# A decode step of attention and feed-forward: half-length result rows stored by ScalarE, block transposes on VectorE, and wo in one load

## The chip, the cores and the metric

One core of one Trainium2 chip. The metric is the device time of one execution in microseconds (us); lower is better. The profiler also gives a *span*, from the first to the last recorded instruction of the program; the time is longer than the span by what the chip does ahead of it and behind it.

## The reference

One token for each of two sequences passes through a transformer block whose layer norms are modulated by a condition `c`. All tensors are bf16; D = 640, 32 heads of 192, the last 1024 of 4096 cached keys and values, F = 1536.

```
mod = (silu(c) @ w_mod).reshape(2, 6, 1, 640)        # sa, ca, ga, sb, cb, gb
h = layernorm(x) * (1 + ca) + sa
x = x + ga * attention(h, k_cache, v_cache, wq, wo)
h = layernorm(x) * (1 + cb) + sb
x = x + gb * ((gelu(h @ w_gate) * (h @ w_up)) @ w_down)
```

## The kernel before

Every weight and every cached key and value is read once, through one arena in SBUF and one queue of loads issued by SyncE. A load is issued as soon as what its place held is consumed; waits for semaphores are worked out from a list of reads and writes. Results with one row for each sequence are laid out as four blocks of 160 columns at partitions 32i, with sequence b at partition 32i + 16b: so TensorE can run four products at once, one at each of its four column positions (in the trace the four matmuls of a round start within 0.01 us of each other).

The parts that the change touches (cuts marked with ...):

```python
WO_SPLIT = [(0, 39), (39, 9)]                         # wo in two loads
...
def f(e):                                             # LN output to columns: 20 small matmuls, then a cast
    hv = hrow[:, :].rearrange("p (m j) -> p m j", j=KT)
    for j in range(KT):
        for i in range(NR):
            last = e.matmul(ps[32*i:32*i+32, BK_M, CT+2*j:CT+2*j+2], lhsT=hv[:, :, j], rhs=selrow[:, i, :], ...)
S.op("dve", lambda e: e.tensor_copy(out=dst_bf[:, :, :], in_=ps[:, BK_M, CT:CT+2*KT]...), ...)
...
keep_clock(9, "clock0")                               # matmuls whose only use is to keep TensorE's clock up
for ci, (t0, n) in enumerate(WO_SPLIT):               # attention output @ wo: 96 matmuls of 320 columns
    ...
    for bk, lo, w in ((2, 0, NA), (3, NA, NA)):
        last = e.matmul(ps[32*i:32*i+B, bk, 0:w], lhsT=oT[:, t, :], rhs=wv[:, tl, lo:lo+w], ...)
# wS <- PSUM by ScalarE and VectorE, then a product with selw sums the four blocks into rows
...
wk = wv[:, k, :].rearrange("p (m i r) -> p i m r", i=NR, r=FR)      # gate and up read runs of 3 of every 12
last = e.matmul(ps[32*i:32*i+B, bk, 0:FT]..., lhsT=h2T[:, k, :], rhs=wk[:, i, :, :], ...)
...
for i in range(NR):                                   # down: 48 matmuls of 160 columns
    last = e.matmul(ps[32*i:32*i+RM, BK_OT, CY:CY+DR], lhsT=aT[:, fc, :], rhs=wv[:, i, :], ...)
S.op("dve", ... fin = ps * modR[:, 5, :]); S.op("dve", ... finb = fin + X)
S.dma("sp", k_dma(out[:, 0, :].rearrange("b (i n) -> i b n", i=NR), finb[0:P:RB, :]), sem_out, ...)
...
S.emit("sp", nc.sync, tail=lambda e: e.wait_ge(sem_out, 16))        # SyncE waits for the store
```

## Time and profile before

| | us |
|---|---|
| time, median of 3 runs | 185.97 (185.91 to 186.12) |
| span of the profiled run | 184.9 |
| last weight landing (semaphore record) | 182.05 |
| from there to the end of the span | 2.8 |

The profile is read in three steps, whose lines stand in the prediction below. The row of DMA activity says whether the stream of loads ever pauses. The chain that ended last, in order of time, says what stands behind the last landing. The timeline of the last 20 us says what runs beside the end of the stream and how long each piece waits; a figure in brackets is idle time ahead of a piece, with what ended it. One more record is used, though no view prints it: each load raises its semaphore in 16 parts (16 records for each load in these traces), which are read here as one for each of the core's 16 DMA engines. A consumer waits for all 16.

### The profile page before, as it was taken

The page shows a single profiled execution, that of the slowest core. Times are in us where ns is not written, and L with a number is a line of the kernel's source. Part 1 is how long each engine was busy: PE and PEld are TensorE (multiplying, and loading weights), DVE is VectorE, ACT ScalarE, POOL GpSimd, SP SyncE. Part 2 cuts the span into 40 slices and gives each one's busy share as a digit, 9 for nine tenths or more (in the row PEclk, how much of TensorE's full clock was granted, in tenths as well). Part 3 has the DMA queues.
Part 4 walks back from the last instruction along what each step waited for, and adds up shares of the span by engine and source line. Part 5 has one row for each costly group of instructions (what it writes and reads, how often), then busy time and mean ns, then how long its engine had stood idle before and what let it go on. Part 6 is the DMA issues. An engine that isn't in the chain of part 4 may idle for free.

```text
span 184.9 us, 1610 instructions
## 1 busy us (share of the span) xinstructions
PE 104.3 (56%) x843; PEld 26.1 (14%) x552; DVE 106.8 (58%) x97; ACT 14.5 (8%) x28; POOL 6.7 (4%) x29
## 2 busy tenths in 40 slices
PE   0015400937666096662598667748663299866853
PEld 0011000020000000001360002400000266411211
DVE  6213000039996489965994999387995649302311
ACT  2032100060000000001000000100000100220410
POOL 7700000000000000000000000000000000000000
PEclk9999999996999759998599999987999669999999
DMA  9999998999897999999898989899999989899980
GB/s 349 433 495 425 425 425 362 429 425 495 367 511 340 511 404 447 457 394 479 374 479 365 500 351 500 383 468 436 425 450 394 491 367 486 378 388 435 419 365 28
DMA packets 2626, 76.97 MB, mean 416 GB/s; under 512 B 314, under 2 KB 444, under 8 KB 572
## 3 DMA queue, kind: packets, MB, share of 16 engines
q1 hardware_dynamic: 2604, 76.88, 96.9%
q8 instruction: 5, 0.08, 0.2%
q14 instruction: 1, 0.01, 0.0%
q10 hardware_dynamic: 16, 0.01, 0.0%
HBM read 76.88 MB, written 0.00 MB: 416 GB/s over the span
## 4 chain that ended last, share of the span: by engine, by line
DMA 57%; DVE 22%; PE 17%; ACT 1%; issue 1%; SPq 0%
DMA arena<-in_A_k_cache_dram 36%; DMA arena<-in_B_w_down_dram 14%; DVE arena L518 12%; DMA arena<-in_w_mod_dram 8%; PE ps L581 8%; DVE S_sb L537 6%; PE ps L530 5%; DVE Em L567 2%; PE ps L470 2%; DVE negm L547 1%; ACT E_sb L555 1%; PE ps L558 1%; DVE M L543 0%; PE ps L551 0%; SPq L287 0%
## 5 line engine op out<-in xcount | busy, mean ns | idle before, releaser
L530 PE MATMUL ps<-arena,ident_b 128*128 128x512 bf16 x192 | 50.7, 411 | 30.2 <-DVE arena L518 30.1
L518 DVE TENSOR_TENSOR arena<-arena,qbc 128x3072 bf16<-128x3072 bf16 x32 | 54.8, 1749 | 11.1 <-DMA arena<-in_A_k_cache_dram 11.1
L581 PE MATMUL ps<-arena,Em 128*64 128x384 bf16 x256 | 24.5, 357 | 5.6 <-DVE Em L567 5.6
L537 DVE TENSOR_REDUCE S_sb<-ps 128x32 f32<-128x1024 f32 x16 | 19.5, 1219 | 8.4 <-PE ps L530 8.4
L581 PEld LDWEIGHTS ps<-arena,Em 128*64 128x64 bf16 x256 | 15.4, 121 | 29.8 <-DVE Em L567 22.2
L567 DVE TENSOR_TENSOR Em<-E_sb,maskE 128x2048 bf16<-128x2048 bf16 x8 | 18.0, 2282 | 2.6 <-PE ps L581 2.6
L492 PE MATMUL ps<-arena,hT 128*2 128x512 bf16 x60 | 4.7, 485 | 11.7 <-DMA arena<-in_A_wq_dram 11.7
L502 DVE CAST qrow<-ps 128x512 bf16<-128x512 f32 x1 | 0.7, 693 | 15.6 <-PE ps L492 15.6
L545 PEld LDWEIGHTS ps<-ident_f,M 128*1 128x1 f32 x2 | 0.2, 80 | 61.5 <-DVE M L543 61.5
L555 ACT ACTIVATE E_sb<-S_sb,nbias 128x256 bf16<-128x256 f32 x2 | 1.0, 507 | 69.3 <-DVE nbias L553 69.3
L651 DVE COPY arena<-ps 128x320 f32<-128x320 f32 x1 | 0.5, 491 | 10.1 <-PE ps L643 10.1
L643 PE MATMUL ps<-arena,oT 128*2 128x320 bf16 x96 | 3.9, 299 | 2.4 <-DMA arena<-in_A_wo_dram 2.4
L588 ACT ACTIVATE On<-ps,rden 128x384 bf16<-128x384 f32 x2 | 1.2, 582 | 47.5 <-PE ps L581 47.5
L403 PE MATMUL ps<-ident_b,crow 2*128 2x2 bf16 x5 | 0.4, 177 | 7.9 <-POOL zsel L383 7.9
L678 PE MATMUL ps<-arena,h2T 128*2 128x384 bf16 x40 | 3.8, 455 | 1.7 <-DMA arena<-in_B_w_up_dram 1.4
L470 PE MATMUL ps<-arena,scT 128*17 128x480 bf16 x40 | 4.3, 597 | 0.5 <-DMA arena<-in_w_mod_dram 0.5
L415 PE MATMUL ps<-Em,ident_b 128*128 128x512 bf16 x17 | 4.2, 379 | 0.2 <-issue 0.2
L408 DVE CAST X<-xr 128x160 f32<-128x160 bf16 x1 | 0.2, 244 | 6.1 <-DMA xr<-in_A_x_dram 6.1
L687 DVE TENSOR_TENSOR aR<-ps,gl 128x384 bf16<-128x384 f32 x1 | 0.6, 558 | 5.4 <-PE ps L678 5.4
L424 PE MATMUL ps<-st,selstat 128*128 128x2 f32 x4 | 0.9, 298 | 4.9 <-ACT sqj L420 4.9
L478 DVE TENSOR_SCALAR opc<-modR 128x160 f32<-128x160 f32 x2 | 0.5, 245 | 5.1 <-ACT modR L475 5.1
L492 PEld LDWEIGHTS ps<-arena,hT 128*2 128x2 bf16 x20 | 0.6, 100 | 15.8 <-issue 15.8
(89 smaller groups left out, 52.6 us busy)
## 6 DMA issues: line engine op xcount, KB each, us to landing
arena<-in_A_v_cache_dram SPq DMA_DIRECT2D x4, 6144.0 KB, 27.2
arena<-in_A_k_cache_dram SPq DMA_DIRECT2D x3, 6144.0 KB, 36.0
arena<-in_A_wq_dram SPq DMA_DIRECT2D x1, 7680.0 KB, 31.3
arena<-in_A_wo_dram SPq DMA_DIRECT2D x1, 6240.0 KB, 27.0
arena<-in_A_k_cache_dram SPq DMA_DIRECT2D x2, 3072.0 KB, 42.7
arena<-in_w_mod_dram SPq DMA_DIRECT2D x1, 4800.0 KB, 14.0
arena<-in_B_w_gate_dram SPq DMA_DIRECT2D x1, 1920.0 KB, 20.7
arena<-in_B_w_up_dram SPq DMA_DIRECT2D x1, 1920.0 KB, 22.7
```

Source lines behind the costliest of these rows:

```text
L415: last = e.matmul(ps[:, BK_T, :], lhsT=ident_b[:, :], rhs=Em[:, 0, 0:512 // H, :].rearrange("p j h -> p (j h)"), start=True, stop=True)
L470: last = e.matmul(ps[32 * i:32 * i + RM, half, 0:MH].rearrange("p (m n) -> p m n", n=DR), lhsT=scT[:, k, :], rhs=wv[:, 3 * half:3 * half + ...
L492: last = e.matmul(ps[32 * i:32 * i + B, n, :], lhsT=hT[:, k, :], rhs=wv[:, kk, i, n * QW:(n + 1) * QW], start=(k == 0), stop=(k == KT - 1) ...
L518: S.op("dve", lambda e: e.tensor_tensor(out=kt, in0=kt, in1=qbc[:, b, :].unsqueeze(1).broadcast_to([P, JC, Dh]), op=ALU.mult), reads=[("qb ...
L530: last = e.matmul(o_ap, lhsT=ident_b[:, :], rhs=kt[:, :, t * GC:(t + 1) * GC], start=(t == 0), stop=(t == NCH - 1))
L537: S.op("dve", lambda e: e.tensor_reduce(out=S_sb[:, b, 2 * JC * pair:2 * JC * (pair + 1)], in_=ps[:, 2 * z:2 * z + 2, :].rearrange("p k (j ...
L547: S.op("dve", lambda e: e.tensor_reduce(out=negm[:, b, :].rearrange("p (h x) -> p h x", x=XQ), in_=ps[0:1, BK_T, 0:P].rearrange("p (h x) - ...
L555: S.op("act", lambda e: e.activation(out=E_sb[:, b, :], in_=S_sb[:, b, :], func=ACTF.Exp, scale=SCALE, bias=nbias[:, b:b + 1], accum_out=d ...
L567: S.op("dve", lambda e, z=z, j=j: e.tensor_tensor(out=Em[:, z, :, :], in0=E_sb[:, b, j:j + JE].unsqueeze(2).broadcast_to([P, JE, H]), in1= ...
L581: last = e.matmul(ps[64 * i:64 * i + 2 * H, BK_O, 0:ON], lhsT=Em[:, z, 2 * jp:2 * jp + 2, :].rearrange("p j h -> p (j h)"), rhs=view(it, l ...
L643: last = e.matmul(ps[32 * i:32 * i + B, bk, 0:w], lhsT=oT[:, t, :], rhs=wv[:, tl, lo:lo + w], start=(t < NR), stop=(t >= NT - NR), tile_po ...
L678: last = e.matmul(ps[32 * i:32 * i + B, bk, 0:FT].rearrange("p (m r) -> p m r", r=FR), lhsT=h2T[:, k, :], rhs=wk[:, i, :, :], start=(k == ...
```

## The change

The intent: fewer steps between the last landing and the end, and fewer instructions for moving rows to columns. Each result row of 160 columns is halved, so that the last two VectorE instructions work on 80 columns and 16 partitions are stored instead of 8; ScalarE, idle by then, issues the store and waits for it. The 32x32 block transposes of VectorE replace small products and casts. wo comes in one load and its product accumulates rows directly, without the later sum.

```diff
-    WO_SPLIT = [(0, 39), (39, 9)]
+    WO_SPLIT = [(0, NT)]
...
-            S.op("pe", f, reads=["hrow", "selrow"], writes=[bank(BK_M)], name=tag + "_T")
-            S.op("dve", lambda e: e.tensor_copy(out=dst_bf[:, :, :], in_=ps[:, BK_M, CT:CT + 2 * KT]...
+            S.op("dve", lambda e: e.transpose(dst_bf[:, :, :], hrow[:, :].rearrange("p (m j) -> p j m", j=KT)),
...
+        def out_rows(src, key, dst_t, name):          # for gb (early) and x (beside gate): rows to half rows
+            S.op("dve", lambda e: e.stream_shuffle(sqj[:, :], src, [...]), ...)
+            ...two products with 0/1 columns...
...
-        keep_clock(9, "clock0")
+        keep_clock(31, "clock0")
...
+            for t in range(NT):
+                for i in range(NR):
+                    last = e.matmul(ps[32 * i:32 * i + RM, 2, 0:DR], lhsT=oT[:, t, :], rhs=wv[:, t, i, :], ...)
...
-                            last = e.matmul(... lhsT=h2T[:, k, :], rhs=wk[:, i, :, :], ...)
+                            last = e.matmul(... lhsT=h2T[:, k, 0:RM:2], rhs=wv[:, k, i * FT:(i + 1) * FT], ...)
...
+        S.op("dve", lambda e: e.transpose(aT[:, RB:RB + FC * 32], aR[:, :]), ...)
...
-                    for i in range(NR):
-                        last = e.matmul(ps[32 * i:32 * i + RM, BK_OT, CY:CY + DR], lhsT=aT[:, fc, :], rhs=wv[:, i, :], ...)
+                    for h, a, m in ((1, 0, OM), (0, RB, GM)):
+                        for i in range(NR):
+                            last = e.matmul(ps[32 * i:32 * i + m, BK_OT, CY:CY + OC], lhsT=aT[...], rhs=wv[:, i, h, :], ...)
...
-        S.dma("sp", k_dma(out[:, 0, :].rearrange("b (i n) -> i b n", i=NR), finb[0:P:RB, :]),
+        S.dma("act", k_dma(out[:, 0, :].rearrange("b (u n) -> u b n", n=OC), finb[0:P:SB, :]),
...
-        S.emit("sp", nc.sync, tail=lambda e: e.wait_ge(sem_out, 16))
+        S.emit("sp", nc.sync)
-        S.emit("act", nc.scalar)
+        S.emit("act", nc.scalar, tail=lambda e: e.wait_ge(sem_out, 16))
```

The order of F behind gate and up changes with it: each block reads 384 contiguous weight columns, and the step of 12 moves to the reads of PSUM by ScalarE and VectorE.

## The prediction

> **What bounds the kernel now.** I read the page first: its slices, then the chain that ended last.
>
> ```profile
> DMA  9999998999897999999898989899999989899980
> GB/s 349 433 495 425 425 425 362 429 425 495 367 511 340 511 404 447 457 394 479 374 479 365 500 351 500 383 468 436 425 450 394 491 367 486 378 388 435 419 365 28
> HBM read 76.88 MB, written 0.00 MB: 416 GB/s over the span
> DMA 57%; DVE 22%; PE 17%; ACT 1%; issue 1%; SPq 0%
> ```
>
> The queues are full from the first slice to the last but one. The chain walks through DVE and PE in the middle, but no slice of the DMA row there falls under 7 tenths, so those steps delay no byte: the kernel is one stream of 76.88 MB, and the time is the stream's end plus what follows the last landing. That tail is the end of the chain in order of time (start, length, what):
>
> ```profile
> 155.58 26.07 DMA arena<-in_B_w_down_dram
> 181.65 0.04 issue
> 181.70 0.39 PE ps L706 x12
> 182.08 0.01 issue
> 182.09 0.28 PE ps L706 x4
> 182.37 0.02 issue
> 182.39 0.34 DVE fin L711
> 182.73 0.02 issue
> 182.75 0.33 DVE finb L713
> ```
>
> The third piece of w_down lands at 182.05 (the trace's record of its semaphore), four matmuls and two vector instructions follow, then the store. The third view is the timeline of the last 20 us, for what runs beside the stream's end (start, length, engine, line, work, idle before and its releaser):
>
> ```profile
> 164.80 2.89 PE L643 MATMUL ps<-arena,oT 128*2 128x320 bf16 x78 [1.78 <-DMA arena<-in_A_wo_dram]
> 168.27 0.98 PE L643 MATMUL ps<-arena,oT 128*2 128x320 bf16 x18 [0.58 <-DMA arena<-in_A_wo_dram]
> 169.28 0.49 DVE L651 COPY arena<-ps 128x320 f32<-128x320 f32 x1 [10.08 <-PE ps L643]
> 170.45 0.33 DVE L664 TENSOR_TENSOR lnt<-ps,modR 128x160 f32<-128x160 f32 x1 [0.67 <-PE ps L657]
> 173.01 0.38 DVE L442 SCALAR_TENSOR_TENSOR hrow<-lnt,rstd,modR 128x160 bf16<-128x160 f32 x1
> 174.09 1.91 PE L678 MATMUL ps<-arena,h2T 128*2 128x384 bf16 x20 [0.27 <-DVE h2T L455]
> 177.45 1.91 PE L678 MATMUL ps<-arena,h2T 128*2 128x384 bf16 x20 [1.45 <-DMA arena<-in_B_w_up_dram]
> 179.49 0.56 DVE L687 TENSOR_TENSOR aR<-ps,gl 128x384 bf16<-128x384 f32 x1 [5.45 <-PE ps L678]
> 180.65 0.73 PE L706 MATMUL ps<-arena,aT 128*17 128x160 bf16 x32 [0.31 <-DVE aT L697]
> 183.10 0.69 SPq L287 DMA_DIRECT2D out_dram<-finb  x1
> ```
>
> The chain wo, LN, gate waits only for wo's second load at 168.27; the up product waits 1.45 us for its weights; the first w_down product (180.65) waits for aT, its weights having landed at 180.52. So there is slack of 1.45 us ahead of up, and after up of about 0.4 us: the first 32 down matmuls end at 181.38, the second piece lands at 181.65.
>
> **What the Trainium skill says.** "DMA: Bandwidth & Descriptors", section "Where 436 GB/s comes from", puts the ceiling at 435 GB/s; here 76.88 MB over 182.05 us is 422, so the stream has no rate left to win. The same page, "Issuing engines are not separate DMA queues", says a copy issued by ScalarE runs on the same 16 engines: moving the store gains at most issue time. "VectorE: DVE Perf Modes", section on the TRN2 errata, gives (N+151)/0.96 ns for an fp32 tensor_tensor; N=160 makes 324 ns, and the trace has 325. The same page, "The three transpose paths", has 311 ns for a VectorE block transpose of 128x128 bf16; the kernel before has none, so only the chip can confirm it.
>
> **The change part by part.**
>
> *wo in one load.* Removed: one load. wq, also 7680 KB but in one load, landed 18.14 us after its predecessor (13.99 to 32.13); wo's two landed 18.24 us after theirs (149.99 to 168.23). So the stream, and every landing after it, moves by -0.10 us. Added: all of wo's products come after the landing at about 168.13. They are now 192 of 160 columns, four at a time at the four column positions, 48 rounds. The down products of before have that form (160 columns, 17 weight columns, a load each): a round every 0.069 us and 0.25 us to the end of the last. So 48 x 0.069 + 0.25 = 3.5 us, from 168.17 to about 171.7, where before the last 18 were done at 169.25.
>
> *Rows summed in PSUM.* Removed: the eviction to SBUF and the selecting product, 169.25 to 170.45, 1.20 us. The multiplication by the gate starts at about 171.7 instead of 170.45: the chain is 1.25 us late.
>
> *Block transposes.* For LN's output, 20 small matmuls and a cast (173.40 to 174.09, 0.69 us with the handovers) become one transpose of 160 columns. From 311 ns for 128 columns at one element a cycle of 0.96 GHz (133 ns) the fixed part is 178 ns, so my estimate is 345 ns, 0.42 us with handovers. Gate starts at 173.40 + 1.25 + 0.42 = about 175.1 instead of 174.09. For the FFN, three matmuls and a cast (180.05 to 180.63) become a transpose of 384 columns, estimated the same way at 0.58 us: no gain.
>
> *Gate and up read whole rows.* Before, each read picked runs of 3 elements out of every 12: 20 matmuls in 1.91 us. wo's contiguous 320-column rounds came every 0.136 us, 0.42 ns a column, so 384 columns make 0.163 us; five rounds and 0.33 us to the end of the last give about 1.0 us (estimate). Each product loses 0.9 us. Gate ends at about 176.1, where it ended before at 176.0, and up waits for its weights at 177.31 as before. Up then ends at 178.35 instead of 179.4. With 0.56 for the gated product and 0.58 + 0.1 for the transpose, aT is ready at about 179.6, and w_down's first piece lands at 180.42: now the weights, not aT, release the down product.
>
> *Down in halves of 80 columns.* 96 matmuls with a load each instead of 48. The small transposing matmuls of before came four every 0.04 us; at that pace the first piece takes 16 x 0.04 + 0.2 = 0.84 us and ends before the second lands (181.55). Behind the last landing (181.95) stand two rounds instead of one, each shorter: 0.25 us, as before.
>
> *Last vector pair.* Two instructions of 80 instead of 160 columns: (80+151)/0.96 = 241 ns for 325, twice, -0.17 us. This is on the path. The two shuffles with their pairs of half-row products run beside the wait for wq and beside gate; VectorE idles 5.45 us there.
>
> *Store by ScalarE.* The SyncE issue took 0.69 us, and the store landed 1.03 us later. ScalarE's two issues at the start took 0.54 and 0.61 us for simpler patterns, where SyncE took 0.33 to 0.39 for its two-dimensional ones. My estimate for 16 rows on ScalarE is 0.75 us, +0.06. The landing stays at about 1.03.
>
> *Head.* Seven GpSimd selections go, LN1's transpose is shorter; all of it ends long before wq lands at 32.1. Zero.
>
> Sum on the path: -0.10 (stream) -0.17 (vector pair) +0.06 (issue) = -0.21 us; 185.97 - 0.21 = 185.76, predicted **185.75 us**, span about 184.6.
>
> **The rivals.**
>
> *wo's chain becomes the bound.* It starts only at the landing. For: 1.25 us late at the gate multiplication. Against: the shorter gate product and 1.3 us of wait for the up weights swallow it. Only at a half clock would it show: wo 6.6, gate and up 2 us each and no wait between make aT ready near 183.7 and the time about 189. The change fills the wait with 31 clock keepers of 0.216 us each, to about 167.7, so I expect full clock. If the gated product, which now reads PSUM with a step of 12, took double, 0.4 us more would still fit ahead of the landing at 180.42.
>
> *A straggling DMA engine.* Each load reports in 16 parts; of the last, the first part came at 179.93 and the last at 182.05. The page lists
>
> ```profile
> q8 instruction: 5, 0.08, 0.2%
> ```
>
> five packets of 16 KB of instructions, and after each, one part of the following loads arrives 1.2 to 1.5 us later relative to the first. The changed program has about 256 more TensorE instructions, so one packet more. If it meets an engine already behind, the end moves by up to 0.4 us: 186.15. Most engines are at 0 to 0.7 us, where it is hidden by the 2.1 of the slowest.
>
> *Much larger gain.* 2% is 3.7 us; the whole stretch from the last landing to the end of the span is 2.8 us. It would take fewer bytes, and there are none fewer.
>
> *ScalarE's store costs or saves more.* By 0.2 us either way; 185.55 to 185.95.
>
> **Range and chances.** The runs of before spread 0.2 us; issue, straggler and stream may each be off by some tenths. Range 185.2 to 186.3. Faster by 2% needs what the tail doesn't hold: 0.01. Slower by 2% needs the half clock or an unforeseen stall in the longer wo chain: 0.02. Within 2%: 0.97.
>
> **What would show it.** w_down's last landing at about 181.95; wo's 192 matmuls in 3.3 to 3.5 us after one wait; gate and up in about 1.0 us each; up and down both released by DMA; the last two vector instructions at 0.24 us; the ScalarE issue at 0.7 to 0.8. Wrong would be: down released by VectorE, a last landing over 182.3, an issue over 1 us, or a store landing much quicker than 1.03 us.

## The result

The changed kernel took 186.01 us (median of 6 runs, 185.83 to 186.11), the kernel before 185.95 in the same rounds. The ratio is 1.0002, with a 95% interval of 0.9989 to 1.0014: no difference. In us that interval reaches from -0.20 to +0.26, so the time alone hardly tells the predicted -0.21 from none at all; what tells them apart is the split into span and rest below. Ratios here are the mean time of one kernel's fast runs over that of the other's of the same rounds, so not quite the ratio of the medians quoted.

Yet the span is shorter: 184.4 to 184.6 us in its six runs. The profile shows most steps where they were expected. First the page of the changed kernel, the DMA row and the queue that fetches instructions:

```profile
DMA  8999998999898989999998989898999999979991
...
q8 instruction: 6, 0.10, 0.2%
```

The stream is as unbroken as before, and there are six instruction packets for five. Next the chain of the changed kernel that ended last:

```profile
155.29 26.18 DMA arena<-in_B_w_down_dram
...
181.52 0.75 PE ps L675 x32
...
182.29 0.25 DVE fin L681
...
182.57 0.24 DVE finb L683
```

The last pieces of w_down still end the stream, with the third landing at 181.88; the two vector instructions behind it take 0.24 us each for 0.33. Then the timeline of the changed kernel over the stretch shown of before:

```profile
168.09 3.50 PE L634 MATMUL ps<-arena,oT 128*17 128x160 bf16 x192 [0.59 <-DMA arena<-in_A_wo_dram]
...
171.64 0.33 DVE L641 TENSOR_TENSOR lnt<-ps,modR 128x160 f32<-128x160 f32 x1 [12.70 <-PE ps L634]
...
174.63 0.35 DVE L439 STREAM_TRANSPOSE h2T<-hrow 128x160 bf16<-128x160 bf16 x1
...
175.04 0.99 PE L655 MATMUL ps<-arena,h2T 128*9 128x384 bf16 x20 [0.65 <-DVE h2T L439]
...
177.29 0.99 PE L655 MATMUL ps<-arena,h2T 128*9 128x384 bf16 x20 [1.26 <-DMA arena<-in_B_w_up_dram]
178.40 0.56 DVE L664 TENSOR_TENSOR aR<-ps,S_sb 128x384 bf16<-128x384 f32 x1 [2.51 <-PE ps L655]
178.99 0.58 DVE L667 STREAM_TRANSPOSE aT<-aR 128x384 bf16<-128x384 bf16 x1
...
180.46 0.76 PE L675 MATMUL ps<-arena,aT 128*25 128x80 bf16 x64 [2.19 <-DMA arena<-in_B_w_down_dram]
...
182.84 0.67 ACTq L290 DMA_DIRECT2D out_dram<-finb  x1
```

wo's product starts only with the landing and takes 3.50 us; the gate multiplication starts at 171.64 instead of 170.45; the transposes take 0.35 and 0.58; gate and up take 0.99 instead of 1.91, and their shapes show 9 weight columns where before had 2. Gate therefore ends at the same time as before, up still waits for its weights (1.26 us), and the down product, which VectorE released in the profile above, now waits for its weights as well.

So the span fell, by about 0.2 us, and the time did not. The experiments ask two questions: where these 0.2 us went, and whether each part did what the prediction says of it.

### The profile page after: what moved, and what is told of

Same layout as the page of the kernel before. It is cut to its first block, busy times and chain, and to the rows that moved or that the text cites. A ratio compares the mean times of both kernels' runs of the same rounds, so it can differ in the third digit from the quotient of the medians.

```text
span 184.6 us, 1862 instructions
## 1 busy us (share of the span) xinstructions
PE 105.9 (57%) x960; PEld 27.5 (15%) x693; DVE 107.4 (58%) x105; ACT 14.4 (8%) x27; POOL 6.1 (3%) x23
## 4 chain that ended last, share of the span: by engine, by line
DMA 59%; DVE 22%; PE 17%; ACT 1%; issue 1%; SPq 0%
DMA arena<-in_A_k_cache_dram 37%; DMA arena<-in_B_w_down_dram 14%; DVE arena L512 12%; DMA arena<-in_w_mod_dram 8%; PE ps L575 8%; DVE S_sb L531 6%; PE ps L524 5%; DVE Em L561 2%; PE ps L454 2%; DVE negm L541 1%; ACT E_sb L549 1%; PE ps L552 1%; DVE M L537 0%; PE ps L545 0%; SPq L290 0%
## 5 line engine op out<-in xcount | busy, mean ns | idle before, releaser
L524 PE MATMUL ps<-arena,ident_b 128*128 128x512 bf16 x192 | 49.6, 401 | 29.4 <-DVE arena L512 29.3
L486 PE MATMUL ps<-arena,hT 128*2 128x512 bf16 x60 | 6.3, 606 | 14.2 <-DMA arena<-in_A_wq_dram 14.2
L408 PE MATMUL ps<-Em,ident_b 128*128 128x512 bf16 x41 | 9.3, 379 | 0.0
L634 PEld LDWEIGHTS ps<-arena,oT 128*17 128x17 bf16 x192 | 3.3, 91 | 7.4 <-DMA arena<-in_A_wo_dram 7.4
L634 PE MATMUL ps<-arena,oT 128*17 128x160 bf16 x192 | 3.5, 233 | 0.6 <-DMA arena<-in_A_wo_dram 0.6
L655 PE MATMUL ps<-arena,h2T 128*9 128x384 bf16 x40 | 2.0, 327 | 1.9 <-DMA arena<-in_B_w_up_dram 1.3
L675 PE MATMUL ps<-arena,aT 128*25 128x80 bf16 (+1 forms) x96 | 1.5, 222 | 2.5 <-DMA arena<-in_B_w_down_dram 2.5
```

The lines of the kernel that those rows point to most:

```text
L408: last = e.matmul(ps[:, BK_T, :], lhsT=ident_b[:, :], rhs=Em[:, 0, 0:512 // H, :].rearrange("p j h -> p (j h)"), start=True, stop=True)
L486: last = e.matmul(ps[32 * i:32 * i + B, n, :], lhsT=hT[:, k, 0:RM:RB], rhs=wv[:, kk, i, n * QW:(n + 1) * QW], start=(k == 0), stop=(k == K ...
L524: last = e.matmul(o_ap, lhsT=ident_b[:, :], rhs=kt[:, :, t * GC:(t + 1) * GC], start=(t == 0), stop=(t == NCH - 1))
L634: last = e.matmul(ps[32 * i:32 * i + RM, 2, 0:DR], lhsT=oT[:, t, :], rhs=wv[:, t, i, :], start=(t == 0), stop=(t == NT - 1), tile_position ...
L655: last = e.matmul(ps[32 * i:32 * i + GM, bk, 0:FT], lhsT=h2T[:, k, 0:RM:2], rhs=wv[:, k, i * FT:(i + 1) * FT], start=(k == 0), stop=(k == ...
```

## Experiments

All were run beside the kernel before, in rounds: twelve runs in three groups, each group on a chip of its own. "Span" is the mean over the timed runs, which record it to 0.1 us, and "rest" is mean time minus mean span. No ratio comes near the 2%. Only for the row with runs of 3 and 9 keepers does the interval leave out 1.

| kernel | time, median | span | rest | ratio (95%) |
|---|---|---|---|---|
| changed kernel, first | 186.01 | 184.55 | 1.45 | 1.0002 (0.9989 to 1.0014) |
| before again | 186.04 | 184.78 | 1.27 | 1.0001 (0.9987 to 1.0015) |
| changed, SyncE waits | 185.88 | 184.64 | 1.27 | 0.9993 (0.9981 to 1.0006) |
| changed, SyncE stores and waits | 185.93 | 184.66 | 1.28 | 0.9995 (0.9983 to 1.0008) |
| before, ScalarE waits | 186.21 | 184.74 | 1.43 | 1.0008 (0.9995 to 1.0020) |
| changed, 9 keepers | 186.20 | 184.78 | 1.44 | 1.0012 (0.9998 to 1.0026) |
| changed, runs of 3 | 186.02 | 184.60 | 1.44 | 1.0005 (0.9989 to 1.0020) |
| changed, full rows | 186.15 | 184.76 | 1.43 | 1.0011 (0.9998 to 1.0023) |
| changed, two loads | 186.10 | 184.68 | 1.42 | 1.0006 (0.9993 to 1.0019) |
| changed again | 186.05 | 184.62 | 1.41 | 0.9999 (0.9986 to 1.0012) |
| changed, SyncE waits, again | 185.88 | 184.72 | 1.29 | 0.9996 (0.9982 to 1.0009) |
| changed, runs of 3 and 9 keepers | 187.10 | 185.63 | 1.48 | 1.0055 (1.0032 to 1.0077) |
| changed, 512 more matmuls | 186.02 | 184.62 | 1.44 | 0.9999 (0.9987 to 1.0010) |

The kernel before, run in the same rounds as each group, had spans of 184.77, 184.72 and 184.81 and a rest of 1.26, 1.27 and 1.28. The first four rows after the first are the first group, the next four the second, the last four the third; spans are best compared within a group. Against the kernel before of its own rounds, the changed kernel's span is shorter by 0.19 us (changed again) and that of the versions in which SyncE waits by 0.09 to 0.13.

### Where the shorter span went: four runs

**The kernel before against itself**, no edit.

> Control: the kernel before, unedited, against itself, so that its span is known for many runs and not for one. In the profiled runs the changed kernel's span was 184.6 us against 184.9, yet the times were 186.01 against 185.95, so the time behind the span grew from about 1.2 to 1.4 us. Theory 1 (the wait for the store, which moved to ScalarE, makes the program's closing sequence longer) and theory 2 (the longer TensorE program does) both expect spans of 184.7 to 184.9 here, time minus span 1.15 to 1.25. Theory 3 (the shorter span of the changed kernel is chance) expects spans that reach down to 184.4 to 184.6 here as well. Ratio 1.000 under all.

Spans of 184.6 to 185.0 in 5 runs, rest 1.27. The spans of the two kernels overlap, so one profile of each would prove little, but the means differ (184.78 here; 184.55 and 184.62 for the changed kernel): theory 3, chance, is not needed for them. And the rest is steady enough to be a measurement.

**The changed kernel with SyncE waiting.**

```diff
-        S.emit("sp", nc.sync)
+        S.emit("sp", nc.sync, tail=lambda e: e.wait_ge(sem_out, 16))
-        S.emit("act", nc.scalar, tail=lambda e: e.wait_ge(sem_out, 16))
+        S.emit("act", nc.scalar)
```

> The changed kernel with one edit: ScalarE still issues the store, SyncE waits for it at the end. Theory 1 (the engine that waits last sets the length of the closing sequence): span stays at 184.6, time minus span falls from 1.44 to 1.2, time 185.75 to 185.8, ratio about 0.999. Theory 2 (the longer TensorE program): time minus span stays at 1.44, time 186.0. Theory 3: span anywhere from 184.4 to 184.9.

Rest 1.27 for 1.45: theory 1. The span is within the spread, and the median fell to 185.88.

**The changed kernel with SyncE storing and waiting**: the same edit, and `S.dma("act", ...out...)` becomes `S.dma("sp", ...out...)`.

> The changed kernel with the store issued and waited for by SyncE, as before. Theory 1: time minus span 1.2; the issue takes about 0.69 us as in before and 0.67 on ScalarE, so the span is within 0.05 us of 184.6 and the time 185.75 to 185.85. Theory 2: time minus span 1.44, time 186.0. If the store by ScalarE is worth something of its own, the span is 0.1 us or more over that of the run in which only the wait moved.

Rest 1.28. The issue took 0.75 us against 0.67 by ScalarE, but from the issue's end to the end of the span, which the store's landing brings, it was 1.05 against 1.10: together 1.80 against 1.77. Who issues the store is worth 0.03 us in these profiles; who waits for it is worth 0.17.

**The kernel before with ScalarE waiting**: SyncE still issues the store, and the wait moves the other way.

> The kernel before with one edit: SyncE issues the store, ScalarE waits for it at the end. Theory 1: span 184.85 as before, time minus span rises from 1.2 to 1.44, time 186.1 to 186.2, ratio about 1.001. Theory 2: time minus span stays at 1.2, time 185.95, ratio 1.000.

Rest 1.43, with none of the changed program's work in it: theory 2 falls. What the longer rest consists of is in the trace too. Behind the last instruction the records show several updates of one semaphore, and then one update of each of over 200 others. I read them as a handshake of the engines and a resetting of semaphores. In the profiled runs in which SyncE waited (before twice, and the two edits above) that resetting starts 0.24 to 0.25 us after the end of the span, behind four updates of the first semaphore, and the last record comes at 1.43 to 1.44; in the two in which ScalarE waited (the changed kernel and this one) at 0.34, behind five updates, and at 1.59. (Every later profile has 0.34 and 0.24 again; the last record came later in one of each, 1.68 and 1.52.) The 0.15 us are part of the closing sequence, and its start shows one update more, 0.09 to 0.10 us behind the fourth. Which engine makes it, and why a late ScalarE needs it, the records do not say.

### The parts of the change

**9 clock keepers instead of 31.**

```diff
-        keep_clock(31, "clock0")
+        keep_clock(9, "clock0")
```

> The changed kernel with 9 clock keepers before wo in place of 31. TensorE then idles from about 162.7 to 168.1, 5.4 us. If the long wait cools the clock (first rival of the prediction), wo's 192 matmuls take 5 to 6.6 us instead of 3.5, gate starts 1.5 to 3 us later at 176.6 to 178.2, up is then released by the gate product and not by its weights, and the span grows by 0 to 1.5 us, since the slack behind up is about 1 us. If the clock stays granted, wo takes 3.5 us and the span stays at 184.6.

The timeline of this run, and the mean granted clock of its stretches (the third figure from the end of the line; before it busy time and instructions of each engine, behind it the share and rate of the DMA):

```profile
168.51 5.36 PE L634 MATMUL ps<-arena,oT 128*17 128x160 bf16 x192 [5.61 <-DMA arena<-in_A_wo_dram]
...
177.32 1.80 PE L655 MATMUL ps<-arena,h2T 128*9 128x384 bf16 x40 [0.65 <-DVE h2T L439]
...
180.87 0.76 PE L675 MATMUL ps<-arena,aT 128*25 128x80 bf16 x64 [1.75 <-DMA arena<-in_B_w_down_dram]
```

```profile
168.00:172.00 4.00, 3.49 (x108) 3.49 (x112) 0.00 (x0) 0.00 (x0) 0.00 (x0) 0.50 0.97 415
```

After 5.61 us of idleness the clock is 0.50 and wo takes 5.36 us for 3.50. That agrees with the Trainium skill's "TensorE: Matmul & The Clock Gate", Part 1: half rate after an idle window of about 3.4 us. But no such window passed wholly idle here: the trace's clock record falls at 165.6, 2.7 us after the last keeper ended at 162.9. Gate starts 2.3 us later and up follows it without a wait for weights. Even so the down product is released by its weights: the slack holds. The profiled span, 185.0, is long because the last landing came at 182.29, the 16th part 2.35 us behind the first; the mean of the runs, 184.78, is 0.05 over the kernel before in the same rounds and 0.16 over the changed kernel run again, which was measured on another chip. I count this within my expectation (0 to 1.5) but it is near what the stragglers alone do.

**Reads in runs of 3 again** (the columns go to the wrong places; the diff is shortened). Its output is wrong, which doesn't matter for the time.

```diff
-  rhs=wv[:, k, i * FT:(i + 1) * FT],
+  rhs=wv[:, k, :].rearrange("p (m i r) -> p i m r", i=NR, r=3)[:, i, :, :],
```

> The changed kernel with one part undone: gate and up read runs of 3 out of every 12 weight columns again (wrong result on purpose, the columns go to the wrong place). If the read pattern alone made the old gate and up products slow, both take 1.9 us again instead of 0.99, up ends at 179.2, aT is ready at about 180.5 and the down product is released by VectorE or nearly at the same time by its weights (180.35), and the span stays within 0.15 us of 184.6: the faster reads buy slack, not time. If it was the two weight columns or another thing, gate and up stay at 1.0 us. If these reads were on the path, the span grows by the 0.9 us of up.

```profile
175.02 1.92 PE L656 MATMUL ps<-arena,h2T 128*9 128x384 bf16 x20 [0.65 <-DVE h2T L439]
...
177.27 1.91 PE L656 MATMUL ps<-arena,h2T 128*9 128x384 bf16 x20 [0.33 <-DMA arena<-in_B_w_up_dram]
...
180.53 0.76 PE L676 MATMUL ps<-arena,aT 128*25 128x80 bf16 x64 [1.35 <-DVE aT L668]
```

1.92 and 1.91 us: the pattern of the read alone made the old products slow, not the number of weight columns (9 here; with 17, in the run with full rows below, contiguous reads take 0.99 too). Now VectorE releases the down product again, as in two of the three profiles of the kernel before, 0.2 us after its weights had landed (180.32), and the end does not move. The contiguous reads bought slack.

**Both taken away**: the two edits together, with a wrong result again.

> The changed kernel with both reserves taken from wo's late chain: reads in runs of 3 (wrong result on purpose) and 9 keepers. Each alone left the span where it was. If the slack is finite as I sum it: wo 5.36 us to 173.6, gate from 177.0 to 178.9 at 1.91, up to 180.8, the gated product 0.56 and the transpose 0.58 with handovers make aT ready at 182.1 to 182.2, the down product takes 1.1 to 1.2 us for its 96 matmuls, and the end moves by 1.2 to 1.5 us: span 185.8 to 186.2, time 187.2 to 187.7, ratio 1.006 to 1.009. If the end is held by the stream all the same, the span stays at 184.6 to 184.8.

```profile
167.96 5.39 PE L634 MATMUL ps<-arena,oT 128*17 128x160 bf16 x192 [5.40 <-DMA arena<-in_A_wo_dram]
...
176.81 3.65 PE L656 MATMUL ps<-arena,h2T 128*9 128x384 bf16 x40 [0.65 <-DVE h2T L439]
...
181.80 1.04 PE L676 MATMUL ps<-arena,aT 128*25 128x80 bf16 x96 [1.35 <-DVE aT L668]
```

This is the edit that moved the time. VectorE releases the down product at 181.80, 1.5 us after its first weights and at the very landing of its last ones, and all 96 matmuls come behind that. From the last landing to the first of the two vector instructions it is 1.13 us for 0.42. The span of this run grew to 185.2 and the mean to 185.63, 1.0 more than the changed kernel in the same rounds. My sum was 0.35 us too late for the down product, and the range that I gave (185.8 to 186.2) holds only two of the four runs, 186.1 and 186.2; the other two have 185.0 and 185.2. The sign and, in the profiled run, the mechanism hold. The profile is of one of the two shorter runs, so what adds another 1 us in the longer ones is not shown. wo's late chain in the changed kernel is affordable because of two other parts of the change, and either alone suffices.

**Full rows again**: 160 columns on 8 partitions, 48 down matmuls, no shuffles, stored by ScalarE (the diff is shortened).

```diff
-  for h, a, m in ((1, 0, OM), (0, RB, GM)):
-      for i in range(NR): last = e.matmul(ps[32*i:32*i+m, BK_OT, CY:CY+OC], ...)
+  for i in range(NR): last = e.matmul(ps[32*i:32*i+RM, BK_OT, CY:CY+DR], lhsT=aT[:, RB+32*fc:RB+32*fc+RM], rhs=wv[:, i, :], ...)
-  fin = ps[..., 80] * go;   finb = fin + xo
+  fin = ps[..., 160] * modR[:, 5, :];   finb = fin + X
```

> The changed kernel with result rows of 160 columns on 8 partitions again (48 down matmuls, no shuffles), still stored by ScalarE. By my sum the half rows are worth 0.17 us in the last two vector instructions: these go from 0.24 to 0.325 us each, the span rises to 184.75 to 184.8 and the time to 186.15. If the two rounds in place of one behind the last landing eat the gain, last landing to the first of these instructions is 0.34 us here against 0.41 in the changed kernel, and the span rises by 0.1 or less. The issue of the store stays at 0.67 us if the engine sets it, and rises or falls by 0.05 us or more if the shape does.

```profile
182.18 0.32 DVE L677 TENSOR_TENSOR fin<-ps,modR 128x160 f32<-128x160 f32 x1 [2.73 <-PE ps L672]
182.53 0.32 DVE L679 TENSOR_TENSOR finb<-fin,X 128x160 bf16<-128x160 f32 x1
182.89 0.59 ACTq L290 DMA_DIRECT2D out_dram<-finb  x1
```

The two vector instructions are back at 0.32 us; from the first of them to the issue of the store it is 0.71 us against 0.55 in the changed kernel, so -0.16 for the half rows. The issue, however, takes 0.59 us here and 0.67 with half rows: 16 partitions cost 0.08 more than 8 on the same engine, so the shape sets part of it (SyncE's issues, 0.69 and 0.75 us, differ in the same direction). From the last landing to the end of the span: 2.82 us here, 2.74 with half rows; the profile's own span, 184.6, is short only because its last landing came early, at 181.77. My 0.34 us from landing to the first of these was a miss: it is 0.41 here. It had come from the one profile of the kernel before in which TensorE was at full clock at the end; in two later profiles of that program it was 0.41 as well.

**wo in two loads again**, with 9 keepers as before.

> The changed kernel with wo in two loads of 39 and 9 rows again, and 9 keepers as before it. By the prediction the stream then ends 0.1 us later: between the landing of the last v piece and that of wo 18.24 us instead of 18.34 in the profiled run of the changed kernel is already against me, so the opposing theory is that the number of loads does not matter and the end of the stream is set by the slowest of the 16 parts, which differs by 0.2 us from run to run whatever the kernel. Prediction: span 184.7, time 186.1. Opposing: span 184.55 to 184.65 as in the changed kernel, with the last landing between 181.75 and 182.05. In both, wo ends about 2 us earlier and the only effect is a longer wait of up for its weights.

```profile
164.74 2.32 PE L636 MATMUL ps<-arena,oT 128*17 128x160 bf16 x122 [1.72 <-DMA arena<-in_A_wo_dram]
...
172.86 0.99 PE L657 MATMUL ps<-arena,h2T 128*9 128x384 bf16 x20 [0.86 <-DVE sqj L469]
...
177.38 1.77 PE L657 MATMUL ps<-arena,h2T 128*9 128x384 bf16 x20 [3.53 <-DMA arena<-in_B_w_up_dram]
...
180.58 1.79 PE L677 MATMUL ps<-arena,aT 128*25 128x80 bf16 x96 [1.42 <-DVE aT L669]
```

wo's product ends 2.4 us earlier and the gate product runs 2.2 us earlier, and nothing follows from it: TensorE then waits 3.53 us for the weights of up, the clock record falls at 175.0, 1.2 us into that wait, and up takes 1.77 us for 0.99, so that VectorE releases the down product again. An early chain that ends in the same wait is of no use here and even costs clock. The number of loads matters a little: taken on the first of the 16 parts, which no straggling touches, wo landed 18.20, 18.21 and 18.27 us after the last v piece in three profiles of the program before (one of them with the wait moved) and 18.22 here, but 18.13 to 18.20, mean 18.15, in the ten profiles with one load. So -0.07 for the one load, where I had 0.10; on the last part the spread from run to run hides it.

### The straggling engines

**512 matmuls of one column more**, in the wait for wq.

```diff
+  for _ in range(512):
+      e.matmul(ps[:, BK_T, 0:1], lhsT=ident_b[:, :], rhs=ident_b[:, 0:1], start=True, stop=True)
```

> The changed kernel with 512 matmuls of one column added while TensorE waits for wq: two more packets of 16 KB of instructions, nothing else of weight. If each such packet puts one of a load's 16 parts behind (second rival of the prediction), the last load shows 8 parts over 0.9 us behind the first instead of 6; the end moves only if a packet meets a part that is behind already: span 184.5 to 185.6, most likely within 0.2 of 184.6. If the packets have nothing to do with it, 6 parts are behind as before. If the added work delayed the stream itself, the first part of the last load would arrive later than 179.75 to 179.95.

```profile
q8 instruction: 8, 0.13, 0.3%
```

In this run 7 packets of 16 KB came ahead of the end of the stream, 5 in the changed kernel; each kernel has in addition one of 8 KB on another queue. Of the 16 parts of the last load, 8 came more than 1.2 us behind the first, where 5 or 6 do in the thirteen other profiles. That fits an instruction packet that puts one part behind, each a different one. The loads of six profiles, taken one after another, support it: the time behind the first part, summed over a load's 16 parts, stays level from load to load and rises by 1.0 to 1.8 us at almost every packet (in the kernel before against itself, one packet shows no rise). Which engine carried a packet is not recorded. The middle of the parts moved from 180.25 to 180.85 (180.18 to 180.46 in the other profiles), but the last part, 2.04 us behind, did not, and neither did the time. Followed from load to load by their order, the parts suggest that the last is an engine that was 0.7 to 0.8 us behind from the first load on and met one packet; no run tests that. The changed kernel's sixth packet came at 181.48, when its parts had all but landed.

**The changed kernel again, and with SyncE waiting again**, on the same chip in the same rounds.

> The changed kernel, unedited, on the same chip and in the same rounds as the version in which SyncE waits. From the earlier runs: span 184.5 to 184.65, time minus span 1.44, time 186.0 to 186.1, ratio 1.000.

> The changed kernel with ScalarE issuing and SyncE waiting for the store, a second time: the version that should beat both. Expected from the sum of the parts measured so far: span 184.55 to 184.65, time minus span 1.27, time 185.85 to 185.9, ratio to the kernel before 0.999 to 0.9995, an interval that may still hold 1.000. If the earlier 0.12 us was chance, the time is that of the changed kernel.

The medians are 186.05 and 185.88, the kernel before 186.10. The rest is 1.41 and 1.29, as expected. But one of the six runs with SyncE waiting took 186.57 with a span of 185.3, so its mean span, 184.72, is no shorter than the changed kernel's, and the interval of the ratio, 0.9982 to 1.0009, holds 1. Twice the median was the lowest of its group; in these rounds it is 0.17 us under the changed kernel's, but the mean only 0.03. A version that clearly beats both it is not.

## Why the prediction was right

The verdict, no difference of 2%, came true by a wide margin, and 186.01 lies in the range, 0.26 us over the 185.75 named. That the two times agree to 0.06 us in the same rounds, though, is not the predicted gain of 0.21 us; see the step that failed, below. By its steps:

- **The stream bounds it, and the tail is small.** Right: the last weights release the last product in both kernels, and no experiment but the one that exhausted the slack moved the mean time by more than 0.25 us from the kernel before. Two readings in it are off. By its own figures (181.38 and 181.65) the slack behind up is 0.27 us and not 0.4. And "no rate left to win" is too strong: from 422 to the page's 435 GB/s is 3% of the stream, by an estimate from these two figures some 5 us; the change does not reach for it. (The section's lower figure for transfers from HBM, about 358 GB/s, does not bind here: 422 is above it.)
- **wo in one load, -0.10.** Right in kind; 0.07.
- **wo's chain 1.25 us late, hidden.** It was 1.19 us late (171.64 for 170.45) against the one profile that the prediction read. In the other two profiles of the kernel before the clock fell just as wo's product began (at 164.9 and 165.0; it took 5.11 us there) and the multiplication starts at 170.99 and 171.01: late by 0.6 only. The keepers have a price too: in the profile of "SyncE waits" they run into wo's landing (167.95) and hold its product back to 168.79, which up's wait hides as well. That the late chain is hidden, and that the shorter gate product and the keepers hide it, is shown by taking each away and both.
- **Transposes 0.345 and 0.58 us.** 0.355 and 0.578 on the chip: the estimate from the skill's 311 ns and one element per cycle holds within 3%.
- **Gate and up 1.0 us.** 0.99.
- **Last vector pair -0.17.** -0.16. It is the largest true gain.
- **Two rounds behind the last landing cost nothing.** Nearly: the second round starts 0.04 us later, and the smaller matmuls end sooner. At a granted clock of 0.50 the first vector instruction starts 0.43 us after the last landing with two rounds (changed again) and 0.41 with one (full rows). What goes with the larger differences is the granted clock: that instruction came 0.35 us after the last landing in the two edits in which gate and up ran late (granted clock 0.96 and 1.00 from 181 to 182.5), and 0.41 to 0.44 in the changed kernel and the other edits but the one with both reserves taken away (0.50 to 0.71). The kernel before shows both: 0.34 at a clock of 1.00 in one profile, 0.41 in the two others, where the clock fell at 182.0. No run sets the clock on purpose there.
- **Issue by ScalarE +0.06.** Too high: 0.67 us for 0.69, with a landing 0.04 us slower.
- **The straggling engine.** Supported: two packets more went with two or three parts more behind, and the end did not move. The extra packet of the changed kernel came too late to do even that.

The step that failed is the last line of the sum, "185.97 - 0.21 = 185.76". It carried a change of the span over to the time one to one. The span did fall, by about 0.2 us (means 184.55 and 184.62 for 184.72 to 184.81); but moving the wait for the store to ScalarE lengthened the rest by 0.13 to 0.18 us, in the closing sequence behind the span. The profile of before could not show it, since its span ends with that wait, and the prediction never asked what follows. The rest of the sum is right, and so the gain of the tail was paid back outside the profile's span. That the two cancel is a coincidence of size: the mechanism of the large terms was right, the equality of the times was luck.

One thing is left open: whether a few keepers between up and down, which would hold the clock for the last product, give the 0.06 us that the two clock states differ by. It was not run.

## What to carry to other kernels

Where one stream of loads bounds a kernel, ask of each change only two things: does it move the end of the stream, and does it shorten what follows the last landing; everything else moves waits about, and a chain that is made early may only idle and lose its clock. When two changes of one commit hide each other's cost, take them away one by one and then together. And compare time with span: the engine that waits last is part of the program's end, which no view of the span shows.

## What the Trainium skill lacked or had wrong

- Closing sequence: "Runtime: NRT & Kernel Launch", section "The ~15µs preamble/postamble breakdown", lists a barrier and a reset of semaphores behind the kernel. What it lacks is that their length depends on the engine that waits last. With the last wait on ScalarE the time behind and ahead of the span was 1.41 to 1.48 us, with it on SyncE 1.26 to 1.29; in the trace the semaphores' reset began 0.34 and 0.24 to 0.25 us after the span.
- Instruction fetch: "Runtime: NRT & Kernel Launch", section "Instruction fetch mechanics", has blocks of 16 KiB, which the trace confirms (packets of 16384 bytes), and calls the cost of a boundary mostly hidden. In the time of the kernel it was hidden: 186.02 us with two packets more for 186.05. But by the order of the parts each packet seems to have put one of the 16 DMA engines of a saturated stream some 1.2 to 1.5 us behind, and a load counts as landed with its last engine, 1.8 to 2.4 us behind the first.
- Reads with a step by TensorE: "TensorE: Matmul & The Clock Gate" gives no figure for them, and the pages that speak of reads with a step in SBUF, "SBUF — State Buffer" and "Advanced Engine Details and Errata", give none for a matmul. 20 matmuls of 384 columns took 0.99 us contiguous and 1.91 to 1.92 us in runs of 3 of every 12 bf16 elements.
- DMA issue by engine: "DMA: Bandwidth & Descriptors" treats SyncE and ScalarE alike. For this store ScalarE's issue took 0.59 us for 8 rows and 0.65 to 0.68 for 16, SyncE's 0.68 to 0.69 and 0.75; the landing after it came 0.03 to 0.06 us later with ScalarE (1.06 to 1.07 us after the issue's end for 1.02 to 1.03).
- Block transposes by length: "VectorE: DVE Perf Modes", "The three transpose paths", has one size, 311 ns at 128 columns. The runs add 353 to 358 ns at 160 columns and 578 ns at 384, SBUF to SBUF.
